# First part's layer out weights split once and kept in DRAM; a new order of scores, copies and sums at the beginning

## The chip, the cores and the metric

The kernel runs on one core of a Trainium2 chip. The metric is the device time of one execution in microseconds, the median of several runs.

## What is computed

Attention in chunks of 64, then a mixture of four experts (ReLU, weighted by normalised shares), then a gated layer. Cut to what matters:

```python
# q, k, v: (4, 8, 576, 64); chunks of 64 along the sequence
attn = softmax_over_chunk(q_c @ k_c.T / 8)            # eps 1e-9 in the sum
x = (attn @ v_c) -> (2304, 512)
# first part: 4 experts, w1 (4, 512, 1024), w2 (4, 1024, 512)
p = domain_probs / (domain_probs.sum(-1) + 1e-9)
x = sum_e p[:, e] * (relu(x @ w1[e]) @ w2[e])
# second part: w_gate, w_val (512, 1536), w_out (1536, 512)
g = x @ w_gate
out = (g * sigmoid(g) * (x @ w_val)) @ w_out
```

## The kernel before, in words

Every float32 operand of a matrix product is split into a high half h, which ScalarE (ACT) rounds to fp32r, and a low half l = source - h, which GpSimd (POOL) or VectorE (DVE) subtracts. A product is three matmuls: h*h, l*h and h*l. `split` (L103) writes the two halves; its lines are L104 (ACT) and L105 (DVE or POOL).

The 2304 tokens go in three passes of 768. A pass runs the first part's 16 sets of layer in weights (256 hidden columns each). Two sets make a group, so a pass has 8 groups in the first part. After the three passes come the three passes of the second part with 12 sets each. Layer in uses Strassen's seven products a set instead of eight (`PRODUCTS`, L59); the sums of weights that this needs are made by `w_sums` (L327). The first two sets of pass 0 are done plainly, without Strassen (`plain`, L504).

Layer out of a group (`layer2`, L516, the matmuls into y at L525, L527 and L529) runs while the next group's layer in runs: 72 matmuls of 512 columns, 18 after every second pair of products. It needs the group's four chunks of layer out weights, 128 rows x 512 columns each, split.

- Layer in weights: in pass 0 each set's raw weights are loaded (`fetch_w1`), summed on DVE, split, used, and the split halves are stored in DRAM (`make_w`, L342). From the third set of pass 1 on they are loaded split (`load_w`, L349).
- Layer out weights of the first part: in **every** pass `fetch_w2` (L406) loads a raw chunk (256 KB) and `split_w2` (L411) splits it on ACT and POOL into a tile of the pool w2 (7 tiles). The raw tiles have 2 buffers. Of the four chunks the last is split two products into the next group (L777, `W + 2`), since seven tiles do not hold two groups.
- Second part: its weights come as 64-bit numbers. `convert` (L358) turns a piece of 128 x 512 into float32 by operations on DVE, ACT and POOL; `make_set64` (L385) does a set with sums and splits, `make_wo` (L398) a chunk of layer out. They are generators: `run_tasks(2)` advances two of them by a step after each product. Four of the `make_wo` (`early`, L707) are put in at L799, when the last attention block is done in pass 0; the rest follows from the third set of pass 1 on (L801).

The order of every engine's instructions is the order in which this program issues them (`manual_schedule`); each engine and each DMA queue works in order. Nearly all DMAs are issued by SP. Work is put off by counting products: `later(d, f)` runs f after d more products.

The beginning (L594 to L695) does six attention blocks of 128 tokens for pass 0, stage by stage: `att_scores` (scores s on PE, maximum and subtraction on DVE, exponential on ACT), `att_turn` (transposes et, copy on ACT, row sums on DVE), `att_values` (av), `att_out` (transposes xt, high halves and a copy x on ACT, low halves on POOL or DVE). From the fifth round on, the plain products of the first two sets (banks of PSUM "z", "w", "x") stand between. `first_sums` (L302) makes the Strassen sums of the tokens, of four subtractions each two on DVE and two on POOL in turn.

The line that sets the order of stages in a round:

```python
stages((att_values, i - 1), (att_turn, i), (att_scores, i + 1), (att_out, i - 1))
```

## Time and profile before

| | us |
|---|---|
| median of 3 runs | 1325.85 (1323.39 to 1326.48) |
| the profiled execution, its own time | 1329.47 |
| its span, first to last instruction | 1327.7 |
| PE busy with matmuls | 1264.9 (95%) |
| DVE, ACT, POOL busy | 706.7, 549.1, 664.9 |
| mean granted TensorE clock | 0.979 |
| DMA | 296.16 MB, 223 GB/s over the span |

The granted clock is 1 at 2.4 GHz and 0.5 at 1.2 GHz; a mean between the two says how much of a stretch ran at either. PE's busy time counts slow and fast matmuls alike, so a stretch loses time in two ways: PE idle, and PE at the lower clock. Idle time of the other engines costs nothing by itself.

### The profile page before, as it was taken

Reading aid. Unit: us, or ns where it says so; the run is one execution under the profiler, and the core shown is the slowest. Engines: PE = TensorE matmul, PEld = TensorE weight load, DVE = VectorE, ACT = ScalarE, POOL = GpSimd, SP = SyncE. Lnnn points to the kernel's source line nnn. Section 1 sums busy time; section 2 is a strip of 40 time slices with the busy share of each in tenths; the row PEclk is TensorE's granted clock in tenths of the full one; section 3 lists DMA queues with packets and bytes.
Section 4 is the critical chain, followed back from the end, with each engine's and each line's share of the span. In section 5 each row is a group of like instructions: output and inputs, shape, how many; then the busy total and the mean of one; then the engine's idle time right before and its main releaser. Section 6 shows DMA issues by size and latency. Waiting matters only on the chain.

```text
span 1327.7 us, 19890 instructions
## 1 busy us (share of the span) xinstructions
PE 1264.9 (95%) x6724; PEld 1134.7 (85%) x6724; DVE 706.7 (53%) x1113; ACT 549.1 (41%) x1177; POOL 664.9 (50%) x632
## 2 busy tenths in 40 slices
PE   7799999987899899998999999999999999999998
PEld 6688888876788788997898888999999999999997
DVE  5567556465635656576764575344335433453343
ACT  3544444334443444445552444343444334343331
POOL 4644434376637667586675576133545423353231
PEclk8999999988899999999999999999999999999999
DMA  6376765656677686779687868475868775577641
GB/s 192 112 252 201 230 199 171 216 201 211 229 247 251 231 282 200 264 256 320 222 277 276 277 199 284 144 249 198 278 218 298 259 236 176 182 245 262 186 144 48
DMA packets 166885, 296.16 MB, mean 223 GB/s; under 512 B 17776, under 2 KB 43632, under 8 KB 166784
## 3 DMA queue, kind: packets, MB, share of 16 engines
q1 hardware_dynamic: 166752, 294.85, 66.8%
q8 instruction: 54, 0.88, 0.3%
q14 instruction: 47, 0.39, 0.1%
q0 software_dynamic: 32, 0.04, 0.0%
HBM read 219.84 MB, written 74.97 MB: 222 GB/s over the span
## 4 chain that ended last, share of the span: by engine, by line
PE 74%; DMA 6%; DVE 6%; POOL 5%; issue 4%; ACT 3%; SPq 1%; POOLq 0%; DVEq 0%; ACTq 0%
PE y L529 11%; PE y L527 11%; PE y L525 11%; PE lx L476 7%; PE lx L478 7%; PE lx L477 7%; PE lz L476 4%; PE lz L478 4%; PE lz L477 4%; PE lw L476 2%; PE lw L478 2%; PE lw L477 2%; POOL w_made L105 2%; DMA w<-w 2%; DMA raw_wo<-wo 1%
## 5 line engine op out<-in xcount | busy, mean ns | idle before, releaser
L105 POOL TENSOR_TENSOR w<-raw,w 128x512 fp32r<-128x512 f32 (+1 forms) x252 | 270.9, 1088 | 340.7 <-ACT w L104 297.3
L527 PE MATMUL y<-w,hh 128*128 128x512 f32 x792 | 314.9, 398 | 18.5 <-POOL w L105 18.5
L529 PE MATMUL y<-w,hl 128*128 128x512 f32 x792 | 315.4, 398 | 9.0 <-DVE hl L434 9.0
L525 PE MATMUL y<-w,hh 128*128 128x512 f32 x792 | 313.8, 396 | 6.5 <-ACT w L104 6.0
L527 PEld LDWEIGHTS y<-w,hh 128*128 128x128 f32 x792 | 150.0, 189 | 50.5 <-POOL w L105 23.0
L529 PEld LDWEIGHTS y<-w,hl 128*128 128x128 f32 x792 | 150.4, 190 | 42.5 <-DVE hl L434 10.5
L525 PEld LDWEIGHTS y<-w,hh 128*128 128x128 f32 x792 | 150.2, 190 | 36.5 <-ACT w L104 7.2
L108 POOL TENSOR_TENSOR hl<-sg,hh 128x384 fp32r<-128x384 f32 x72 | 79.6, 1112 | 199.4 <-ACT hh L451 191.0
L433 ACT ACTIVATE hh<-sum_p 128x384 fp32r<-128x384 f32 x92 | 48.3, 525 | 283.6 <-DVE sum_p L464 283.6
L464 DVE TENSOR_TENSOR sum_p<-lx,p 128x384 f32<-128x384 f32 x82 | 45.6, 556 | 167.4 <-PE lx L478 167.4
L546 DVE SCALAR_TENSOR_TENSOR acc<-y,prob,acc 128x512 f32<-128x512 f32 x126 | 90.9, 743 | 74.4 <-PE y L529 74.4
L104 ACT ACTIVATE w<-raw 128x512 fp32r<-128x512 f32 (+1 forms) x252 | 128.1, 522 | 3.0 <-DMA raw<-wo 1.9
L434 DVE SCALAR_TENSOR_TENSOR hl<-sum_p,hh 128x384 fp32r<-128x384 f32 x92 | 61.2, 666 | 60.3 <-ACT hh L433 60.3
L105 POOL TENSOR_TENSOR w_made<-raw,w_made 128x256 fp32r<-128x256 f32 x84 | 72.2, 876 | 9.6 <-ACT w_made L104 9.6
L460 ACT COPY u<-lx 128x384 f32<-128x384 f32 x82 | 39.1, 477 | 81.4 <-PE lx L478 81.0
L451 ACT ACTIVATE hh<-sg 128x384 fp32r<-128x384 f32 x72 | 38.0, 528 | 70.8 <-DVE sg L448 70.8
L464 DVE TENSOR_TENSOR sum_p<-lw,p 128x384 f32<-128x384 f32 x82 | 45.3, 553 | 36.5 <-PE lw L478 33.7
L476 PE MATMUL lw<-b21h,w 128*128 128x384 f32 x164 | 56.1, 342 | 6.9 <-DVE hl L434 5.5
L476 PE MATMUL lx<-t2h,w 128*128 128x384 f32 x164 | 56.9, 347 | 3.8 <-ACT p L460 3.7
L476 PE MATMUL lx<-t3h,w 128*128 128x384 f32 x164 | 57.7, 352 | 0.0
L478 PE MATMUL lx<-t3h,w 128*128 128x384 f32 x164 | 57.5, 351 | 0.0
L477 PE MATMUL lx<-t3l,w 128*128 128x384 f32 x164 | 57.4, 350 | 0.0
(233 smaller groups left out, 2842.5 us busy)
## 6 DMA issues: line engine op xcount, KB each, us to landing
w<-w SPq DMA_DIRECT2D x574, 256.0 KB, 4.4
raw<-w SPq DMA_DIRECT2D x96, 256.0 KB, 4.0
w<-w_made SPq DMA_DIRECT2D x84, 256.0 KB, 4.3
raw<-w SPq DMA_DIRECT2D x18, 512.0 KB, 3.9
raw<-wo SPq DMA_DIRECT2D x36, 256.0 KB, 4.6
sums<-x SPq DMA_DIRECT2D x40, 192.0 KB, 4.0
xt<-sums SPq DMA_DIRECT2D x40, 192.0 KB, 2.2
xraw_t<-xt SPq DMA_DIRECT2D x20, 384.0 KB, 4.2
```

What stands on the lines that cost most here:

```text
L104: nc.scalar.activation(h, src, AF.Copy)
L105: (lo or nc.vector).tensor_tensor(out=l, in0=src, in1=h.bitcast(F32), op=ALU.subtract)
L108: (eng or nc.vector).tensor_tensor(out=o, in0=a, in1=b, op=ALU.subtract)
L434: nc.vector.scalar_tensor_tensor(out=l, in0=src, scalar=0.0, in1=h.bitcast(F32), op0=ALU.max, op1=ALU.subtract)
L464: nc.vector.tensor_tensor(out=t, in0=ps, in1=snap.pop(name), op=ALU.add)
L476: nc.tensor.matmul(ps, w[:, 0, c], xh[:, k], start=f, stop=False, skip_group_check=True)
L477: nc.tensor.matmul(ps, w[:, 0, c], xl[:, k], start=False, stop=False, skip_group_check=True)
L478: nc.tensor.matmul(ps, w[:, 1, c], xh[:, k], start=False, stop=e, skip_group_check=True)
L525: nc.tensor.matmul(y, hh[:, c], w[:, 0], start=(j == 0), stop=False)
L527: nc.tensor.matmul(y, hh[:, c], w[:, 1], start=False, stop=False)
L529: nc.tensor.matmul(y, hl[:, c], w[:, 0], start=False, stop=(j == 3))
L546: nc.vector.scalar_tensor_tensor(out=sum_, in0=y, scalar=p, in1=sum_, op0=ALU.mult, op1=ALU.add)
```

## The change

It has three parts.

1. **Layer out weights of the first part.** In pass 0 a chunk, once split, is also stored in DRAM (`w2_d`, both halves, 512 KB), three products after its split. In passes 1 and 2 `fetch_w2` loads the two halves (512 KB) straight into the w2 tile, and `split_w2` does nothing. The tile is therefore taken when the load is issued, no longer at the split. From the last group of pass 0 on, the fourth chunk of every odd group has a tile of its own (`w2x_p`), so two groups fit, and the fourth chunk no longer waits for the next group.
2. **Conversions.** The four `early` conversions of second part layer out leave pass 0 and take their places in the list that starts in pass 1.
3. **The beginning.** Scores of the next block are issued ahead of this block's transposes, and the pieces of `att_scores` and `att_turn` on DVE and ACT are issued in a new order (`att_soft`, `att_sums`, `att_exp`). All four subtractions of `first_sums` go to DVE; the sums, splits and banks behind the plain products stand in a new order.

The diff, cut:

```diff
--- before.py
+++ after.py
@@ -98,6 +98,7 @@
 
     xt_d = [dram.tile([4, P, 2, TT], F32, name=f"xt_{s}") for s in range(2 * NPASS)]
     w_d = [dram.tile([NPROD, P, 2, 2 * P], F32, name=f"w_{n}") for n in range(NPAIRS + 2 * NPAIRS2)]
+    w2_d = [dram.tile([P, 2, DM], F32, name=f"w2_{c}") for c in range(4 * NG1)]
     wo_d = [dram.tile([P, DM], F32, name=f"wo_{c}") for c in range(F2 // P)]
 
     def split(h, l, src, lo=None):
@@ -232,11 +233,23 @@
                 )
         if next_in_place(a) is not None:
             att_load(next_in_place(a))
+        s["s"] = ps
+        if a >= BLOCKS:
+            att_soft(a)
+
+    def att_soft(a):
+        s = att[a]
+        ps = s.pop("s")
         mx = st_p.tile([P, H], F32, tag="mx", name=f"mx{a}")
         pool, how = (acc_p, dict(tag="acc")) if a < BLOCKS else (at_p, dict(tag="e", bufs=3))
         e = s["e"] = pool.tile([P, H, CH], F32, name=f"e{a}", **how)
         nc.vector.tensor_reduce(out=mx, in_=ps, op=ALU.max, axis=AX.X)
         nc.vector.tensor_tensor(out=e, in0=ps, in1=mx.unsqueeze(2).to_broadcast(ps.shape), op=ALU.subtract)
+        if a >= BLOCKS:
+            att_exp(a)
+
+    def att_exp(a):
+        e = att[a]["e"]
         nc.scalar.activation(e, e, AF.Exp, scale=SCALE)
 
     def transpose(ps, src):
@@ -253,6 +266,11 @@
         ps = transpose(att_ps(f"et{a}", where), s["e"])
         et = s["et"] = at_p.tile([P, H, CH], F32, tag="et", name=f"et{a}", bufs=1)
         nc.scalar.copy(et, ps)
+        if a >= BLOCKS:
+            att_sums(a)
+
+    def att_sums(a):
+        s = att[a]
         sm = st_p.tile([P, H], F32, tag="sm", name=f"sm{a}")
         nc.vector.tensor_reduce(out=sm, in_=s["e"], op=ALU.add, axis=AX.X)
         nc.vector.tensor_scalar_add(sm, sm, EPS)
@@ -305,9 +323,9 @@
         b1, b2 = x_first[0, j], x_first[1, j]
         d0, d1 = slice(0, 2), slice(2, 4)
         sub(b1[:, d0], b2[:, d0], b1[:, d0])
-        sub(b2[:, d0], b2[:, d1], b2[:, d0], nc.gpsimd)
+        sub(b2[:, d0], b2[:, d1], b2[:, d0])
         sub(b2[:, d1], b2[:, d1], b1[:, d0])
-        sub(b1[:, d1], b1[:, d1], b2[:, d1], nc.gpsimd)
+        sub(b1[:, d1], b1[:, d1], b2[:, d1])
 
     FIRST_PLACES = {"t1": (0, slice(0, 2)), "t3": (1, slice(0, 2)), "t2": (1, slice(2, 4)), "t4": (0, slice(2, 4))}
 
@@ -404,13 +422,27 @@
     raw2, w2op = {}, {}
 
     def fetch_w2(G, j):
-        part, _, g = part_of(G)
+        part, s, g = part_of(G)
+        if part == 1 and s > 0:
+            t = w2op[G, j] = w2_tile(G, j)
+            nc.sync.dma_start(t.bitcast(F32), w2_d[4 * g + j])
+            return
         r = raw2[G, j] = raw2_p.tile([P, DM], F32, tag="raw2", name=f"raw2_{G}_{j}")
         nc.sync.dma_start(r, w2[4 * g + j] if part == 1 else wo_d[4 * g + j])
 
+    def w2_tile(G, j):
+
+        pool = w2_p if G < NG1 - 1 or G % 2 == 0 or j < 3 else w2x_p
+        return pool.tile([P, 2, DM], F32R, tag="w2", name=f"w2_{G}_{j}")
+
     def split_w2(G, j):
-        t = w2op[G, j] = w2_p.tile([P, 2, DM], F32R, tag="w2", name=f"w2_{G}_{j}")
+        part, s, g = part_of(G)
+        if (G, j) not in raw2:
+            return
+        t = w2op[G, j] = w2_tile(G, j)
         split(t[:, 0], t[:, 1], raw2.pop((G, j)), lo=nc.gpsimd)
+        if part == 1:
+            later(3, lambda: nc.sync.dma_start(w2_d[4 * g + j], t.bitcast(F32)))
 
 
     hid = {}
@@ -465,7 +497,7 @@
         return t
 
     def bank(b, name):
-        return (psX if b == "x" else psL).tile([P, 512], F32, tag=b, name=name)[:, :TT]
+        return {"x": psX, "y": psY}.get(b, psL).tile([P, 512], F32, tag=b, name=name)[:, :TT]
 
     def half_k(ps, w, x, first, last):
 
@@ -635,14 +667,17 @@
             nc.gpsimd.tensor_tensor(out=prob, in0=prob, in1=sm.unsqueeze(2).to_broadcast(prob.shape), op=ALU.mult)
 
         def stages(*some):
-            for stage, a in some:
+            for stage, a, *w in some:
                 if 0 <= a < BLOCKS:
-                    stage(a, where())
+                    stage(a, *w)
+
+
 
         for i in range(-1, BLOCKS + 1):
             if i >= HALF + 1:
                 plain(*pieces.pop(0), "zw"[i % 2])
-            stages((att_values, i - 1), (att_turn, i), (att_scores, i + 1), (att_out, i - 1))
+            stages((att_values, i - 1, where()), (att_scores, i + 1, where()))
+            stages((att_turn, i, where()), (att_soft, i + 1), (att_sums, i), (att_out, i - 1, where()), (att_exp, i + 1))
             if i == 0:
                 shares()
             elif i == 1:
@@ -659,38 +694,37 @@
                 w2_p = ctx.enter_context(tc.tile_pool(name="w2", bufs=7, reuse_waits="tile"))
                 fetch_w2(0, 0)
                 fetch_w2(0, 1)
-            elif i == 6:
-                first_sums(0)
-                first_split("t2", 0)
-                w_sums(raw1[2], nc.gpsimd)
 
         del raw1[0], raw1[1]
         fetch_w1(3)
-        plain(*pieces.pop(0), "x")
-        first_sums(1)
-        first_split("t2", 1)
+        plain(*pieces.pop(0), "w")
+        first_sums(0)
         make_w(2, 0)
         make_w(2, 1)
-        plain(*pieces.pop(0), "x")
+        plain(*pieces.pop(0), "y")
+        first_sums(1)
+        w_sums(raw1[2], nc.gpsimd)
+        first_split("t2", 0)
+        plain(*pieces.pop(0), "y")
         first_sums(2)
+        first_split("t2", 1)
         first_split("t2", 2)
         make_w(2, 2)
+        make_w(2, 3)
+        plain(*pieces.pop(0), "z")
+        for j in range(HALF):
+            first_split("t1", j)
         split_w2(0, 0)
         split_w2(0, 1)
         fetch_w2(0, 2)
         fetch_w2(0, 3)
-        plain(*pieces.pop(0), "z")
-        for j in range(HALF):
-            first_split("t1", j)
-        make_w(2, 3)
-        plain(*pieces.pop(0), "w")
+        plain(*pieces.pop(0), "x")
+        make_w(2, 4)
+        make_w(2, 5)
         for j in range(HALF):
             first_split("t3", j)
-        plain(*pieces.pop(0), "x")
-        make_w(2, 4)
         split_w2(0, 2)
         split_w2(0, 3)
-        make_w(2, 5)
         for j in range(HALF):
             first_split("t4", j)
 
@@ -704,12 +738,9 @@
         tasks, running = [], []
 
         make64 = []
-        early = [make_wo(c) for c in range(4)]
         for q in range(NPAIRS2):
             for m in range(2):
-                make64.append(make_set64(q, m))
-                if 2 * q + m >= 4:
-                    make64.append(make_wo(2 * q + m))
+                make64 += [make_set64(q, m), make_wo(2 * q + m)]
 
         def run_tasks(n):
             while len(running) < n and tasks:
@@ -773,8 +804,9 @@
 
                 W = NPROD * sum(group_of(k) == group_of(n) for k in range(len(sets)))
                 for j in range(4):
+                    last = W + 2 if group_of(n) < NG1 - 1 else 5 + j * W // 4
                     later(1 + j * W // 4, lambda G=group_of(n), j=j: fetch_w2(G, j))
-                    later(5 + j * W // 4 if j < 3 else W + 2, lambda G=group_of(n), j=j: split_w2(G, j))
+                    later(5 + j * W // 4 if j < 3 else last, lambda G=group_of(n), j=j: split_w2(G, j))
             if last_of_pass(n + 1) and i == 5:
                 for k in range(3):
                     x_fetch(p + 1, k)
@@ -794,9 +826,10 @@
                     at_cm.close()
                     y_places.append((psA, "a"))
                     xt_p = ctx.enter_context(tc.tile_pool(name="xt", bufs=3, side="right"))
+                    w2x_p = ctx.enter_context(tc.tile_pool(name="w2x", bufs=1, side="right"))
                     raw64_cm = ExitStack()
                     raw64_p = raw64_cm.enter_context(tc.tile_pool(name="raw64", bufs=2, side="right"))
-                    tasks += [x_sums(1)] + early
+                    tasks.append(x_sums(1))
             if o == (NPAIRS + 2, 1):
                 tasks += [x_sums(2)] + make64
             elif o == (2 * NPAIRS + 3, 1):
```

### Where instructions move

Three places, row by row as the program's order has them. In a row stands the line, the operation, the tile written, the tiles read, and the shape; "x8" is eight in a row.

PE in the beginning, from the first scores on (s scores, et transposed exponentials, av values, xt transposed outputs; plz is the first plain product). Before:

```order
L230 MATMUL s_222<-kbd_158,q_196 64x128 x8
L244 MATMUL et_240<-ident,e_236 128x128 x4
L230 MATMUL s_252<-kbd_160,q_200 64x128 x8
L268 MATMUL av_275<-vbd_159,et_245 64x128 x8
L244 MATMUL et_287<-ident,e_266 128x128 x4
L230 MATMUL s_299<-kbd_162,q_206 64x128 x8
L244 MATMUL xt_313<-ident,e_236 128x128 x4
L268 MATMUL av_334<-vbd_161,et_292 64x128 x8
```

Now:

```order
L231 MATMUL s_254<-kbd_190,q_228 64x128 x8
L231 MATMUL s_272<-kbd_192,q_232 64x128 x8
L257 MATMUL et_285<-ident,e_268 128x128 x4
L286 MATMUL av_307<-vbd_191,et_290 64x128 x8
L231 MATMUL s_319<-kbd_194,q_238 64x128 x8
L257 MATMUL et_328<-ident,e_293 128x128 x4
L257 MATMUL xt_344<-ident,e_268 128x128 x4
L286 MATMUL av_366<-vbd_193,et_333 64x128 x8
```

The next block's scores now stand ahead of this block's et, where they stood behind it.

POOL near the end of pass 0, sets 13 and 14 (raw_5_3 is the last raw chunk of layer out of group 5, raw_6_0 the first of group 6; raw_13 is the layer in weights of set 13; wo a conversion; sums_1_1 the token sums of pass 1). Before:

```order
L380 TENSOR_TENSOR neg_wo_2946<-neg_wo_2946,raw_wo_2887 128x512
L381 TENSOR_TENSOR top_wo_2945<-top_wo_2945,neg_wo_2946 128x512
L105 TENSOR_TENSOR w_5_3_3042<-raw_5_3_2898,w_5_3_3042 128x512
L105 TENSOR_TENSOR w_2_3046<-raw_13_2863,w_2_3046 128x256
L105 TENSOR_TENSOR w_3_3062<-raw_12_2656,w_3_3062 128x256
L105 TENSOR_TENSOR w_5_3086<-raw_13_2863,w_5_3086 128x256
L105 TENSOR_TENSOR w_6_0_3124<-raw_6_0_2999,w_6_0_3124 128x512
```

Now:

```order
L109 TENSOR_TENSOR sums_1_0_2940<-sums_1_0_2940 128x384
L106 TENSOR_TENSOR w_5_3_3087<-raw_5_3_2952,w_5_3_3087 128x512
L106 TENSOR_TENSOR w_2_3091<-raw_13_2916,w_2_3091 128x256
L106 TENSOR_TENSOR w_3_3107<-raw_12_2707,w_3_3107 128x256
L106 TENSOR_TENSOR w_5_3130<-raw_13_2916,w_5_3130 128x256
L106 TENSOR_TENSOR w_6_0_3166<-raw_6_0_3046,w_6_0_3166 128x512
```

The two rows of the conversion ahead of group 5's last split are gone.

SP in pass 1 (w_83, w_84 the stored halves of sets' layer in weights; before: raw_11_1 a raw chunk of layer out, 128x512; now: w_11_0 the split halves of one, 128x1024; wv and wo the 64-bit weights of the second part). Before:

```order
L351 DMA w_5_4756<-w_83 128x512
L409 DMA raw_11_0_4775<-w 128x512
L351 DMA w_0_4777<-w_84 128x512
L360 DMA raw_0_1_4781<-wg 128x1024
L351 DMA w_1_4817<-w_84 128x512
L351 DMA w_6_4830<-w_83 128x512
L409 DMA raw_11_1_4847<-w 128x512
```

Now:

```order
L369 DMA w_5_4729<-w_83 128x512
L428 DMA w_11_0_4749<-w_12_117 128x1024
L369 DMA w_0_4751<-w_84 128x512
L378 DMA raw_1_1_4753<-wv 128x1024
L369 DMA w_1_4788<-w_84 128x512
L369 DMA w_6_4798<-w_83 128x512
L419 DMA wo_138<-top_wo_4697 128x512
L428 DMA w_11_1_4813<-w_13_118 128x1024
```

The load of a chunk keeps its place in the queue; it is twice as large and takes its w2 tile there.

## Rows read from the trace of the kernel before

**Rows 1.** Busy time in eight stretches: window, PE, PEld, DVE, ACT, POOL, clock, DMA share, GB/s

```profile
0.00:14.00 14.00, 9.39 (x69) 8.26 (x70) 6.49 (x15) 3.13 (x4) 7.54 (x20) 0.78 0.72 219
14.00:44.00 30.00, 24.24 (x222) 19.80 (x223) 16.39 (x34) 14.31 (x35) 11.47 (x17) 0.93 0.59 171
44.00:73.00 29.00, 22.34 (x141) 19.96 (x140) 18.82 (x31) 14.50 (x39) 23.88 (x28) 0.88 0.29 92
73.00:240.00 167.00, 167.00 (x1073) 145.08 (x1073) 103.89 (x182) 70.19 (x166) 67.67 (x77) 1.00 0.67 216
240.00:322.00 82.00, 66.52 (x311) 56.88 (x310) 47.20 (x70) 32.16 (x75) 47.46 (x48) 0.92 0.57 196
322.00:380.00 58.00, 53.53 (x254) 47.83 (x253) 32.90 (x43) 25.09 (x55) 35.62 (x32) 0.91 0.72 239
380.00:830.00 450.00, 429.13 (x2114) 382.20 (x2113) 276.74 (x400) 204.12 (x437) 293.45 (x269) 0.98 0.76 257
830.00:1327.00 497.00, 492.71 (x2553) 454.70 (x2551) 204.26 (x343) 185.59 (x369) 177.81 (x145) 1.00 0.63 209
```

**Rows 2.** PE's waits between 240 and 830 us: total us, times, longest

```profile
PE y L527 <- POOL w L105: 17.2, 10, 3.4
PE y L529 <- DVE hl L434: 9.0, 4, 4.2
PE y L525 <- ACT w L104: 6.0, 2, 5.2
```

**Rows 3.** The same waits between 380 and 830 us, one row

```profile
PE y L527 <- POOL w L105: 13.3, 8, 3.4
```

**Rows 4.** Timeline of PE in the beginning: start, us, instruction, [idle before <- releaser]

```profile
14.85 1.09 PE L230 MATMUL s<-kbd,q 128*64 128x128 f32 x16
...
18.71 1.09 PE L230 MATMUL s<-kbd,q 128*64 128x128 f32 x16
...
26.12 0.45 PE L476 MATMUL plz<-b11h,w 128*128 128x384 f32 x1 [1.87 <-ACT b11h L291]
...
63.14 0.69 PE L476 MATMUL lw<-b21h,w 128*128 128x384 f32 x1 [5.47 <-DVE hl L434]
...
72.79 0.50 PE L525 MATMUL y<-w,hh 128*128 128x512 f32 x1
```

**Rows 5.** Timeline of DVE in the beginning

```profile
52.73 0.43 DVE L108 TENSOR_TENSOR x<-x,x 128x256 f32<-128x256 f32 x1 [2.71 <-POOL x L108]
53.70 0.56 DVE L105 TENSOR_TENSOR t2l<-x,t2h 128x256 fp32r<-128x256 f32 x1 [0.54 <-ACT t2h L104]
...
59.90 2.72 DVE L105 TENSOR_TENSOR t1l<-x,t1h 128x256 fp32r<-128x256 f32 x3
```

**Rows 6.** Timeline of ACT in the beginning: the split of a chunk

```profile
64.23 0.94 ACT L104 ACTIVATE w<-raw 128x512 fp32r<-128x512 f32 x2 [0.87 <-DMA raw<-w]
```

**Rows 7.** Timeline of DVE and POOL late in pass 0: a conversion

```profile
309.23 0.43 DVE L367 TENSOR_SCALAR top_wo<-raw_wo 128x512 f32<-128x512 f32 x1 [6.17 <-DMA raw_wo<-wo]
...
271.17 1.51 POOL L380 TENSOR_TENSOR neg_wo<-neg_wo,raw_wo 128x512 f32<-128x512 f32 x1
272.75 1.32 POOL L381 TENSOR_TENSOR top_wo<-top_wo,neg_wo 128x512 f32<-128x512 f32 x1
```

**Rows 8.** Timeline of PE late in pass 0: two of its waits

```profile
275.54 0.49 PE L527 MATMUL y<-w,hh 128*128 128x512 f32 x1 [2.84 <-POOL w L105]
...
315.69 0.80 PE L525 MATMUL y<-w,hh 128*128 128x512 f32 x1 [5.24 <-ACT w L104]
```

**Rows 9.** Groups by line and shape, 380 to 830 us: busy, mean ns | idle before

```profile
L105 POOL TENSOR_TENSOR w<-raw,w 128x512 fp32r<-128x512 f32 x53 | 71.7, 1353 | 111.5 <-ACT w L104 84.1 <-DVE hl L434 15.8 <-DMA w<-w 11.6
...
L104 ACT ACTIVATE w<-raw 128x512 fp32r<-128x512 f32 x54 | 33.4, 619 | 0.0
```

**Rows 10.** DMA issues of the page: the load of split layer in weights

```profile
w<-w SPq DMA_DIRECT2D x574, 256.0 KB, 4.4
```

## The prediction

> **What bounds the kernel now.** I read the windows first [rows 1]. In each row the reader should see two losses of PE: the stretch less PE's busy time, and the stretch times one less the clock (time at 1.2 GHz does half the work, and the mean clock says how much of it there was). From 73 to 240 us PE is never idle and at the full clock; there the kernel is bound by its matmuls, and no edit off PE can gain. From 830 us on it loses 4.3 us, all of it near the end. The losses stand elsewhere:
>
> - 0 to 14 us: idle 4.6, clock 3.1, together 7.7.
> - 14 to 73 us: idle 5.8 + 6.7, clock 2.1 + 3.5, together 18.0.
> - 240 to 322 us: idle 15.5, clock 6.6, together 22.0.
> - 322 to 380 us: idle 4.5, clock 5.2, together 9.7.
> - 380 to 830 us: idle 20.9, clock 9.0, together 29.9.
>
> That is 87 us, and no more than this can be won. Next come PE's waits [rows 2, 3]: between 240 and 830 us the largest is layer out's matmul (y) for a low half of its weights, which POOL writes: 17.2 us in ten waits, 13.3 of it after 380 us. Layer out's other two waits are for a high half on ACT (6.0) and for hidden low halves on DVE (9.0). For the cause of a wait I then looked at the timeline of the engine that releases it [rows 5 to 7].
>
> **The change, part by part.** The sum is made against the profiled execution's own time, 1329.47 us, which is 3.6 above the median of the runs; the forecast takes the same gain off the median.
>
> *The beginning (14 to 73 us).* Before, the scores of the next block stand behind this block's et, which waits for maximum, subtraction and exponential. So a block takes 18.71 - 14.85 = 3.86 us [rows 4]. With the scores ahead of et, DVE and ACT work beside PE, and a block is bounded by PE's four pieces, 1.09 for s as in the row, about the same for av, and under 0.7 each for et and xt: some 3.4 us by estimate. Over five blocks that is 2 us. The stalls at the first plain product (1.87 us idle, [rows 4]) shrink only in part, since its low halves still come from the last xt through ACT and DVE. The token sums go back and forth between DVE and POOL: one wait of DVE for POOL is 2.71 us [rows 5], behind POOL's weight sums. Four subtractions on DVE alone are 4 x 0.43 = 1.7 us a place instead of about 3.2 from one place's first to its last. Three places come 4 to 5 us earlier, and this chain ends at the 5.47 us stall of PE at 63.14 [rows 4] and at the 1.2 GHz stretch behind it, part of the 3.5 us. But the late chunks of layer out are still fetched into two raw buffers behind POOL's splits of the first two, and ACT, which splits them in order ahead of a copy that PE needs, already waits for such a load [rows 6]. With everything earlier that wait grows, and a part of the stall comes back there. So of 18.0 I take **10**; bounds 4 (only the block pace and one short stall) and 14. Nothing in 0 to 14 us is taken: what ends those waits are the first loads.
>
> Here a rule weighs against the move to DVE. Three low halves on DVE took 2.72 us beside POOL's work, 0.91 each, where one by itself took 0.56 [rows 5]. So 12 subtractions and 6 low halves could each be 0.35 longer, 18 x 0.35 = 6 us; the beginning would give 4, and the sum below would be 31 instead of 37. I leave it as a rival, since before the change the POOL pieces of the sums met DVE as well. The Trainium skill says why (SBUF — State Buffer, section "SBUF: two separate sides"): an operation of DVE with two SBUF inputs and one of GpSimd take a shared pair of ports in turn, and whoever comes second is blocked for the whole of the other's instruction. By that rule it is the 31.
>
> *Conversions leave pass 0 (240 to 322 us).* Four conversions stand here. DVE waits 6.17 us in order for the raw load of one [rows 7], and everything behind it, ACT's split of a chunk among it, comes late: PE waits 5.24 us [rows 8]. Two POOL pieces of another, 1.51 + 1.32 us [rows 7], stand right ahead of a chunk's low half, and PE waits 2.84 [rows 8]: the very length of the two. Up to 240 us the same sets without conversions cost PE no wait at all, though there the attention blocks gave POOL and DVE more time a set. Of 22.0 us I take **18**; bounds 11 (clock and the smaller waits stay) and 22. From 322 to 380 us the cause is mostly pass 0's own weight sums on DVE, which stay; I take **2**, bounds 0 and 5.
>
> *Chunks loaded split in passes 1 and 2 (380 to 830 us).* 64 splits go; 53 of POOL's pieces lie in this stretch, 71.7 us of POOL, and 33.4 of ACT [rows 9]. By themselves they cost nothing; what counts is PE's 13.3 us behind them [rows 3] and a like share of the clock loss, 13.3 / 20.9 x 9.0 = 5.7. The fourth chunk no longer stands right ahead of its use. Of 19 I take **14**; bounds 8 (other POOL pieces make the next weights late) and 21 (some of DVE's waits go as well).
>
> *What it adds.* The four conversions now come in passes 1 and 2. Bounds: nothing, as PE's other losses there, 29.9 - 19 = 11 us over 32 pieces of the same kind, are 0.3 a piece; and 22, what four cost late in pass 0. I take **3**, near the rows of their new place. The list of conversions gets longer, not denser: two still run at a time.
>
> DMA: 32 stores of 512 KB in pass 0 and 64 loads larger by 256 KB, 16.8 MB each. At full share the rows give 216 / 0.67 = 322 and 257 / 0.76 = 338 GB/s [rows 1], so 52 and 50 us of the engines' time, spread over about 280 and 500 us: shares of 0.86 or so in both. It fits, but what stands behind such a transfer comes 0.8 us later (0.26 MB at 338 GB/s). If one in four of 64 loads passed that on to PE, 12 us; if none, 0. I take **4**. The stores also put 32 waits for POOL into SP's queue, in a pass whose loads have lasted without a wait of PE from 73 to 240 us; I cost them at nothing there, their cover being the six products by which weights are asked for ahead.
>
> SP: a load now waits for its w2 tile, until 18 matmuls of layer out of two groups before are through. At 497 us for 2553 matmuls [rows 1] those are 3.5 us. Once a group SP is held until then; the split weights behind it have six products of lead and land in 4.4 us [rows 10]. So it is costed at nothing; if the lead is used up, see the second rival. What goes: SP's waits for POOL to free the two raw buffers.
>
> The sum: 10 + 18 + 2 + 14 - 3 - 4 = 37 us. 1329.5 - 37 = 1292.5 for the profiled execution; from the median, 1325.85 - 37 = **1289**.
>
> **The rivals.**
>
> 1. *DVE becomes the beginning's bound*, by the taking of turns above. For it: 0.91 against 0.56 [rows 5]. Against: POOL's share of the sums goes. Beginning 4, sum 31, 1295. Chance 0.15.
> 2. *SP is held and loads come late: slower.* Place: passes 1 and 2, the first chunk of each of 16 groups. If the six products of lead are not there, because SP was late before, each hold passes its 3.5 us on to PE: 16 x 3.5 = 56 us, 1289 + 56 = 1345. It decides from 37 / 16 = 2.3 us a group. For it: the queue is one and in order, and the DMA share rises. Against: loads land in 4.4 us, and SP loses its old waits. Chance 0.08.
> 3. *The conversions take their stalls along.* In passes 1 and 2 they are as dear as in pass 0: 22 instead of 3, sum 18, 1308. For it: POOL and DVE are as busy there, 0.65 and 0.61 of the stretch [rows 1]. Against: 32 such pieces cost PE at most 11 us there now. Chance 0.15.
> 4. *It doesn't do what it says.* PE's next matmuls wait for the next POOL piece in line instead, the 14 are not won, and the conversions take their stalls along: 37 - 14 - 19 = 4, 1322. Chance 0.04.
>
> **How the numbers follow.** The forecast has what is left, 0.58. What a measurement of this kernel can tell from no change is about 0.3%, 4 us. Faster by more than that: forecast, rivals 1 and 3, 0.58 + 0.15 + 0.15 = 0.88. Within it: rival 4, 0.04. Slower: rival 2, 0.08. The range's low end has all upper bounds and nothing added: 14 + 22 + 5 + 21 = 62, so 1264. The high end has the lower bounds with the dear side of what is added, short of the conversions' 22: 4 + 11 + 0 + 8 - 3 - 8 = 12, so 1314. It holds the forecast, rivals 1 and 3, and leaves out rivals 2 and 4, 0.12, and some tails.
>
> **What would show it.** In the profile after:
>
> - the first layer out matmul, at 72.79 before [rows 4], comes near 63; if near 69, rival 1;
> - PE's idle and clock loss in pass 0 after attention is under 5 us, and no wait there is put down to ACT's or POOL's split of a chunk;
> - in passes 1 and 2 no split of 128x512 is left on POOL, and layer out waits for a low half on POOL in the second part at most;
> - PE's waits for DMA of split weights, if any, stay under 5 us in sum; if they stand once a group, rival 2.
>
> The forecast is wrong if PE still loses over 45 us between 73 and 830 us, or if the gain stands where no term puts it.

## The result and the profile after

| | before | after |
|---|---|---|
| median of the runs on this chip, us | 1325.53 (1323.39 to 1326.48) | 1276.95 (1276.67 to 1277.32) |
| the profiled execution, its own time | 1329.47 | 1277.32 |
| its span | 1327.7 | 1275.6 |
| PE busy | 1264.9 (95%) | 1244.0 (98%) |
| POOL busy | 664.9 | 568.5 |
| mean granted clock | 0.979 | 0.993 |
| DMA moved, MB | 296.16 | 329.71 |

The ratio is 0.9636, with a 95% interval of 0.9619 to 0.9652: 48.6 us faster by the medians. The forecast was 1289, from 1264 to 1314: the direction and the range hold, and the gain is 11.6 us larger than the 37 of the sum.

The windows of the profile after, cut as those of before where the place in the program is the same (window, its length, PE, PEld, DVE, ACT, POOL, clock, DMA share, GB/s):

```profile
0.00:14.00 14.00, 10.38 (x104) 8.88 (x106) 8.61 (x18) 4.38 (x8) 7.86 (x20) 1.00 0.75 229
14.00:44.00 30.00, 24.49 (x217) 21.58 (x214) 15.85 (x35) 15.35 (x38) 11.88 (x17) 0.94 0.64 192
44.00:73.00 29.00, 21.61 (x137) 19.40 (x137) 21.83 (x38) 14.31 (x36) 20.41 (x24) 0.88 0.33 95
...
240.00:322.00 82.00, 81.17 (x419) 72.80 (x418) 50.39 (x70) 35.44 (x82) 55.64 (x55) 1.00 0.85 298
322.00:380.00 58.00, 53.48 (x264) 47.23 (x263) 27.42 (x44) 20.49 (x44) 17.73 (x17) 0.94 0.78 279
...
380.00:830.00 450.00, 444.35 (x2226) 399.24 (x2225) 270.23 (x425) 189.54 (x403) 222.57 (x220) 1.00 0.84 301
```

Against [rows 1]: from 240 to 322 us PE's loss falls from 22.0 to 0.8; from 380 to 830 us it falls from 29.9 to 5.7 (450 - 444.35, with the clock at 1.00 to two decimals). The 29.9 is some 2.5 too high: its 9.0 of clock comes from a mean of 0.98 over 450 us, and windows of 50 us give 0.97, 0.97, 0.99 and 0.94 in four of nine and 1.00 in the others, which is 6.5. From 14 to 73 us the idle time and the clock look about as before (18.0 and 18.2 us lost); the first 14 us, of which the forecast took nothing, lose 3.6 instead of 7.7.

The program runs ahead of its old times, so windows alone mislead; places in the program are better. I take the same four places in both timelines: the first matmul of layer out, the last transpose of attention, the stall at the change from pass 0 to 1, and the first sigmoid of the second part. Of PE after:

```profile
62.48 0.69 PE L508 MATMUL lx<-t2h,w 128*128 128x384 f32 x1 [7.39 <-ACT p L492]
...
68.07 0.50 PE L557 MATMUL y<-w,hh 128*128 128x512 f32 x1
...
244.36 0.63 PE L257 MATMUL xt<-ident,e 128*128 128x128 f32 x4 [0.83 <-DVE e L293]
...
331.34 0.79 PE L561 MATMUL y<-w,hl 128*128 128x512 f32 x1 [3.30 <-DVE hl L466]
```

and of ACT after:

```profile
843.39 0.53 ACT L473 ACTIVATE sg<-sum_p 128x384 f32<-128x384 f32 x1
```

In the trace before the first stands at 72.79 [rows 4], the other three here:

```profile
248.65 0.63 PE L244 MATMUL xt<-ident,e 128*128 128x128 f32 x4 [0.83 <-DVE e L275]
...
357.87 0.80 PE L529 MATMUL y<-w,hl 128*128 128x512 f32 x1 [4.23 <-DVE hl L434]
...
894.08 0.53 ACT L441 ACTIVATE sg<-sum_p 128x384 f32<-128x384 f32 x1
```

So the lead is 4.7, then 4.3, 26.5 and 50.7 us, and 52.1 at the end of the span. The differences say where it was won: **beginning 4.3, late pass 0 22.2, passes 1 and 2 24.2, the rest 1.4**. (The traces differ by 52.1 and the medians by 48.6, since the profiled run of before lay 3.9 above its median.)

The 24.2 holds most of that excess. From the stall at the change of pass to the first sigmoid the profiled execution of before takes 536.2 us. Two kernels below that split chunks there just as before, a1_begin and a2_wo, take 529.4 and 529.6 in theirs, and a1_begin's lay 3.1 below its median. The change takes 512.1. So by medians passes 1 and 2 gained some 20, by estimate (24.2 less 3.9).

The waits of PE after, between 380 and 830 us (total us, times, longest), are four, 5.6 us in sum, and have nothing of a weight in them:

```profile
PE y L561 <- DVE hl L466: 2.9, 2, 1.7
PE y L557 <- ACT acc L597: 1.6, 1, 1.6
PE x1t L257 <- DVE acc L578: 0.7, 1, 0.7
PE lx L508 <- ACT p L492: 0.4, 1, 0.4
```

Before, the same stretch had the row for POOL [rows 3] and smaller ones, of which the two largest are:

```profile
PE y L529 <- DVE hl L434: 3.3, 1, 3.3
PE lw L476 <- DMA w<-w: 1.4, 2, 1.1
```

The row for POOL, 13.3 us, is gone, with the splits that made it. It is most of what went: PE's idle time there fell by 15.2 us (20.9 to 5.7), so the other waits fell by 2 in all. SP's queue shows the hold that the second rival feared, L428 waiting for layer out's last matmul, 16 times, as many as passes 1 and 2 have groups, and the same queue's waits for POOL to free raw tiles (164.2 us in 50 times before) shrunk to L431's:

```profile
SPq L369 <- PE lx L510: 93.0, 75, 3.0
...
SPq L428 <- PE y L561: 41.0, 16, 7.6
...
SPq L431 <- POOL w L106: 24.3, 8, 15.6
```

### The profile page after: what moved, and what is told of

Read it like the earlier page. It is cut to its first block, busy times and chain, and to the rows that moved or that the text cites. A ratio compares the mean times of both kernels' runs of the same rounds, so it can differ in the third digit from the quotient of the medians.

```text
span 1275.6 us, 19749 instructions
## 1 busy us (share of the span) xinstructions
PE 1244.0 (98%) x6724; PEld 1123.0 (88%) x6724; DVE 680.9 (53%) x1119; ACT 518.8 (41%) x1113; POOL 568.5 (45%) x562
## 2 busy tenths in 40 slices
DMA packets 171492, 329.71 MB, mean 258 GB/s; under 512 B 18288, under 2 KB 44144, under 8 KB 171392
## 4 chain that ended last, share of the span: by engine, by line
PE 86%; DVE 5%; DMA 3%; ACT 2%; issue 1%; SPq 1%; POOL 1%; DVEq 0%; POOLq 0%; ACTq 0%
PE y L561 13%; PE y L557 13%; PE y L559 13%; PE lx L508 8%; PE lx L510 8%; PE lx L509 8%; PE lz L508 4%; PE lz L510 4%; PE lz L509 4%; PE lw L510 2%; PE lw L508 2%; PE lw L509 2%; PE av L286 1%; PE s L231 1%; ACT hh L465 1%
## 5 line engine op out<-in xcount | busy, mean ns | idle before, releaser
L106 POOL TENSOR_TENSOR w<-raw,w 128x256 fp32r<-128x256 f32 (+1 forms) x188 | 184.9, 1000 | 207.9 <-ACT w L105 178.0
L106 POOL TENSOR_TENSOR w_made<-raw,w_made 128x256 fp32r<-128x256 f32 x84 | 67.6, 814 | 71.4 <-ACT w_made L105 65.0
L105 ACT ACTIVATE w<-raw 128x256 fp32r<-128x256 f32 (+1 forms) x188 | 88.7, 490 | 7.6 <-DMA raw<-w 6.4
L398 POOL TENSOR_TENSOR neg<-neg,raw 128x512 f32<-128x512 f32 x24 | 31.7, 1322 | 113.6 <-DMA w<-w 51.5
L508 PE MATMUL lz<-t1h,w 128*128 128x384 f32 x164 | 56.1, 342 | 0.0
L508 PE MATMUL lx<-t3h,w 128*128 128x384 f32 x164 | 56.0, 342 | 0.0
L510 PE MATMUL lx<-t3h,w 128*128 128x384 f32 x164 | 55.9, 341 | 0.0
```

What stands on the lines that cost most here:

```text
L105: nc.scalar.activation(h, src, AF.Copy)
L106: (lo or nc.vector).tensor_tensor(out=l, in0=src, in1=h.bitcast(F32), op=ALU.subtract)
L508: nc.tensor.matmul(ps, w[:, 0, c], xh[:, k], start=f, stop=False, skip_group_check=True)
L510: nc.tensor.matmul(ps, w[:, 1, c], xh[:, k], start=False, stop=e, skip_group_check=True)
```

## The experiments

My theory after the result was: each of the three parts acts by itself, late pass 0 through the conversions, passes 1 and 2 through the splits, and the beginning gave little because ACT's splits of late chunks stand ahead of a copy that PE needs. Rivals: the chunks' new tile and place rather than the missing splits; DVE slowed by POOL in the beginning; conversions that are dear in their new place; traffic or SP's holds that eat a part of the gain. Eleven kernels were run, in three groups, each beside the kernel before on one chip. A difference "against the change" is taken between medians; as the kernel before had 1326.2 to 1326.5 beside these groups and 1325.5 beside the change, up to 1 us of such a difference can be the chip.

**One part at a time.** The kernel before with the third part of the change (order and sums at the beginning), nothing else:

```diff
+            stages((att_values, i - 1, where()), (att_scores, i + 1, where()))
+            stages((att_turn, i, where()), (att_soft, i + 1), (att_sums, i), (att_out, i - 1, where()), (att_exp, i + 1))
...
-        sub(b2[:, d0], b2[:, d1], b2[:, d0], nc.gpsimd)
+        sub(b2[:, d0], b2[:, d1], b2[:, d0])
```

> The beginning's new order alone; layer out chunks and conversions as before. Theory: the three parts work in separate stretches and add up, and the beginning is worth what the two traces show at the last transposes of attention, 248.65 - 244.36 = 4.3 us: 1321. Rival: it is worth the 10 of the forecast and the other parts take some back: 1315.

Measured: 1320.93 against 1326.5, ratio 0.9960 (0.9940 to 0.9979), about 5.6 us. First layer out matmul and last transpose stand about where they stand in the change (68.0 and 243.9, against 68.07 and 244.36). The beginning is worth about 5, not 10.

The kernel before with the four conversions moved to the list of pass 1:

```diff
-        early = [make_wo(c) for c in range(4)]
...
+                make64 += [make_set64(q, m), make_wo(2 * q + m)]
...
-                    tasks += [x_sums(1)] + early
+                    tasks.append(x_sums(1))
```

> The four conversions moved from pass 0 to passes 1 and 2, nothing else. Theory: the stalls between 240 and 322 us go (22 us) and each conversion costs under 1 us in its new place: 1304 to 1307. Rival: conversions take their stalls along, 5.5 us each: 1320 to 1326.

Measured: 1300.68, ratio 0.9811 (0.9787 to 0.9835), 25.8 us. The windows of this kernel, late in pass 0 and in passes 1 and 2:

```profile
240.00:322.00 82.00, 81.17 (x417) 72.62 (x416) 52.04 (x72) 36.88 (x86) 55.07 (x55) 1.00 0.70 236
...
380.00:830.00 450.00, 433.73 (x2142) 388.25 (x2141) 286.04 (x418) 210.10 (x447) 300.12 (x274) 0.99 0.76 261
```

From 240 to 322 us PE loses 0.8 instead of 22.0. In passes 1 and 2, where four more conversions now run, it does not lose more than before (16.3 idle against 20.9, and against 18.5 in a1_begin, which has the old conversions). The third rival of the prediction falls.

The kernel before with the chunks stored and loaded split (the first part of the change, with its eighth tile):

```diff
+        if part == 1 and s > 0:
+            t = w2op[G, j] = w2_tile(G, j)
+            nc.sync.dma_start(t.bitcast(F32), w2_d[4 * g + j])
+            return
```

> Chunks stored split in pass 0 and loaded split in passes 1 and 2, with the eighth tile; beginning and conversions as before. Theory: passes 1 and 2 gain about 24 us, the stores cost nothing: 1301. Rival: the stores meet the conversions' loads in pass 0 and make their stalls longer, or the gain after 330 us needed the conversions' move: 1308 or more.

Measured: 1303.56, ratio 0.9830 (0.9811 to 0.9848), 22.9 us. Its windows:

```profile
240.00:322.00 82.00, 64.48 (x307) 54.73 (x306) 46.53 (x69) 31.90 (x75) 47.35 (x47) 0.92 0.68 241
...
380.00:830.00 450.00, 445.53 (x2232) 400.90 (x2231) 260.89 (x414) 184.64 (x394) 215.29 (x216) 1.00 0.84 297
```

Late pass 0 keeps its whole loss, while in passes 1 and 2 PE is idle for only 4.5. The three parts give 5.6 + 25.8 + 22.9 = 54.3 by themselves and 48.6 together: nearly additive, each mainly in its own stretch.

**Splits, or the fourth chunk's place?** The change, but passes 1 and 2 load raw chunks and split them; the eighth tile stays, nothing is stored:

```diff
-        if part == 1 and s > 0:
-            t = w2op[G, j] = w2_tile(G, j)
-            nc.sync.dma_start(t.bitcast(F32), w2_d[4 * g + j])
-            return
...
-        if part == 1:
-            later(3, lambda: nc.sync.dma_start(w2_d[4 * g + j], t.bitcast(F32)))
```

> As the changed kernel, but passes 1 and 2 load raw chunks and split them on ACT and POOL, and nothing is stored; the eighth tile stays, so the fourth chunk is split four products after its load and not in the next group. Theory: the work of 64 splits and SP's waits for raw buffers cost most of the gain in passes 1 and 2: 1288 to 1300. Rival: the fourth chunk's late place was the whole of it: 1277 to 1281.

Measured: 1292.38, ratio 0.9750 (0.9731 to 0.9768), 15.4 slower than the change. Its window of passes 1 and 2:

```profile
380.00:830.00 450.00, 433.48 (x2141) 386.06 (x2140) 277.73 (x415) 209.73 (x446) 297.67 (x273) 0.99 0.77 261
```

and the wait that came back in SP's queue:

```profile
SPq L426 <- POOL w L105: 106.1, 39, 15.5
```

PE's wait for POOL's low halves is back too, 5.2 us in 4 waits. The fair comparison for this kernel is a2_wo, which has the same conversions and the same splits without the eighth tile. From the stall at the change of pass to the first sigmoid, a2_wo:

```profile
333.91 0.80 PE L529 MATMUL y<-w,hl 128*128 128x512 f32 x1 [4.43 <-DVE hl L434]
...
863.54 0.53 ACT L441 ACTIVATE sg<-sum_p 128x384 f32<-128x384 f32 x1
```

and this kernel:

```profile
329.46 0.79 PE L554 MATMUL y<-w,hl 128*128 128x512 f32 x1 [3.30 <-DVE hl L459]
...
858.97 0.53 ACT L466 ACTIVATE sg<-sum_p 128x384 f32<-128x384 f32 x1
```

That is 529.6 and 529.5 us: the fourth chunk's new place won nothing there in these two executions. By medians at most some 3 us are left for it, if the other two parts add up (1326.5 - 5.6 - 25.8 = 1295.1). It is the splits that count, with the raw tiles that hold up SP; these two come and go together here, and no run parts them.

**The beginning: POOL beside DVE, or ACT's order?** The change with two of four subtractions back on POOL:

```diff
-        sub(b2[:, d0], b2[:, d1], b2[:, d0])
+        sub(b2[:, d0], b2[:, d1], b2[:, d0], nc.gpsimd)
...
-        sub(b1[:, d1], b1[:, d1], b2[:, d1])
+        sub(b1[:, d1], b1[:, d1], b2[:, d1], nc.gpsimd)
```

> As the changed kernel, with first_sums alternating between DVE and POOL as before. Theory: PE's next matmuls wait for ACT, which waits for late chunk loads, so where the sums run hardly matters: within 2 us of 1277. Rival (DVE is slowed by POOL): faster than 1277 by 2 to 6 us. Other rival (the move was the gain): 1280 or more.

Measured: 1278.99, ratio 0.9642 (0.9627 to 0.9656), 2.0 slower than the change by medians, with overlapping intervals. In the trace the first layer out matmul comes at 70.27, and the wait for ACT's copy is 9.5 us, where it is 7.2 to 8.1 in the seven traces that have the beginning of the change. That DVE meets POOL does cost DVE time (below), but giving POOL the work back is no gain.

The change with the splits of the third and fourth chunk put off behind the first products:

```diff
-        split_w2(0, 2)
-        split_w2(0, 3)
...
+        later(1, lambda: split_w2(0, 2))
+        later(2, lambda: split_w2(0, 3))
```

> As the changed kernel, but chunks 2 and 3 of the first group are split one and two products later, so that ACT's copy which frees the bank no longer stands behind their late loads. Theory: PE's wait of 7.4 us before the third product shrinks to about 4 (the next bound is the exponential of block 6, behind DVE's weight sums), and with it the 1.2 GHz stretch: 1272 to 1274. Rival (the wait only moves to layer out, which needs these chunks): 1276 to 1278.

Measured: 1274.13 (1273.08 to 1275.35), ratio 0.9599 (0.9583 to 0.9615), 2.8 faster than the change: it **beats both kernels**. ACT in the change, ahead of the copy that PE waits for:

```profile
58.98 0.63 ACT L105 ACTIVATE w<-raw 128x512 fp32r<-128x512 f32 x1 [1.84 <-DMA raw<-w]
60.52 0.63 ACT L105 ACTIVATE w<-raw 128x512 fp32r<-128x512 f32 x1 [0.91 <-DMA raw<-w]
61.05 1.01 ACT L105 ACTIVATE t4h<-x 128x256 fp32r<-128x256 f32 x3
61.97 0.46 ACT L492 COPY p<-lx 128x384 f32<-128x384 f32 x1
```

and in this kernel:

```profile
55.98 1.01 ACT L105 ACTIVATE t4h<-x 128x256 fp32r<-128x256 f32 x3
56.90 0.46 ACT L492 COPY p<-lx 128x384 f32<-128x384 f32 x1
```

The copy comes 5 us earlier, PE's longest wait for it falls from 7.4 to 3.4, and the first layer out matmul comes at 65.57. Not all of it is this edit's: the first stretch, to 44 us, went somewhat better in this trace too (25.23 us of PE against 24.49, where the waits for the first loads differ from run to run), and the first layer in product stood 1.1 us earlier ahead of the stall (49.52 against 50.58). So of the 2.5 us at the first layer out matmul some 1.4 are the edit's in this pair of traces.

A third try at the same stall, the first set's layer in weights fetched one attention block later (`if a == 3:` for `if a == 2:`, so that SP sends attention's loads first):

> As the changed kernel, but the first raw weights (512 KB) are asked for behind the fourth block's q and k instead of ahead of them. Theory: the scores of the fourth block, which wait 2.9 us for k, come 1.5 to 2 us earlier, and the 1.2 GHz stretch behind them is shorter: 1273 to 1275 if nothing later takes it back. Rival: it is taken back at the wait for chunks, whose time is set by POOL's splits: 1276.5 to 1278.

Measured: 1279.43 (1276.88 to 1281.22), ratio 0.9640 (0.9621 to 0.9658). The wait for attention's loads went from 4.0 to 2.0, that for ACT's copy to 8.5. In this trace PE ran slower from 14 to 44 us (clock 0.83 against 0.94), and the first layer in product came at 53.75 against 50.58. No gain; why the clock was lower is not shown.

**What the change adds.** Each split chunk loaded twice into its tile, to double the traffic:

```diff
-            nc.sync.dma_start(t.bitcast(F32), w2_d[4 * g + j])
+            for _ in range(2):
+                nc.sync.dma_start(t.bitcast(F32), w2_d[4 * g + j])
```

> As the changed kernel, but each of the 64 loads of split chunks in passes 1 and 2 is issued twice, 33.5 MB more. Theory: the DMA engines have room there (0.85 of the time busy), SP's hold costs nothing, so 64 more loads cost 0 to 8 us: 1277 to 1285. Rival (DMA is at its limit): 33.5 MB at 340 GB/s are 99 us over 510 us, above what is free, and PE pays 20 us or more: 1297 or more.

Measured: 1441.21, ratio 1.0857 (1.0837 to 1.0876), 164 us slower, far from both. The kernel did not test what I meant: the second load writes the tile that the first writes, so SP waits until the first has landed, with everything queued behind it. PE's waits in this kernel:

```profile
PE lx L509 <- DMA w<-w: 64.9, 38, 5.9
PE lz L509 <- DMA w<-w: 15.2, 13, 2.6
PE lw L509 <- DMA w<-w: 10.0, 9, 2.7
```

and the longest of the waits in SP's queue:

```profile
SPq L429 <- DMA w<-w: 375.7, 77, 8.2
```

It is the second rival's mechanism at work, SP held until PE's loads come late: 164 / 64 = 2.6 us for each added load. The waits are only a part of it; the clock from 380 to 830 us is 0.92. In the change SP is held 41.0 us in 16 waits at no cost that a wait of PE shows; held 375.7 us in all, it runs through the lead of six products.

The traffic by itself then: one more load of 256 KB behind each, into a tile that nobody reads, so 16.8 MB more:

```diff
+            u = spare_p[0].tile([P, DM], F32, tag="u", name=f"u_{G}_{j}")
+            nc.sync.dma_start(u, w2_d[4 * g + j][:, 0])
```

> The change, with one more load of 256 KB behind each of the 64 loads of split chunks in passes 1 and 2, into a tile of its own that nobody reads: the 16.8 MB that the change itself adds to loads there, once more, and this time no load waits for the one just ahead of it. Theory (that traffic is hidden, six products of lead are enough): within 3 us of the change, 1274 to 1280, no wait of PE for DMA of weights over 2 us. Rival (the prediction's 4 us for traffic was near, the DMA share of 0.85 leaves little): 4 to 12 us slower, 1281 to 1289, with PE's waits for DMA spread over passes 1 and 2.

Measured: 1281.97 (1278.58 to 1283.64), ratio 0.9658 (0.9634 to 0.9682), 5.0 slower than the change, the single runs 1.6 to 6.7, with overlapping intervals. Neither side is clean. No wait of PE names a DMA of weights, though the DMA share from 580 to 680 us is 0.95. The trace loses most of its time at one spot, the change from pass 1 to 2. The 20 us there in the change, its window and PE's wait:

```profile
680.00:700.00 20.00, 18.32 (x90) 15.99 (x89) 14.41 (x24) 8.07 (x18) 8.84 (x7) 1.00 0.85 310
...
689.84 0.50 PE L561 MATMUL y<-w,hl 128*128 128x512 f32 x1 [1.68 <-DVE hl L466]
```

The same 20 us with the spare loads:

```profile
680.00:700.00 20.00, 16.96 (x67) 13.80 (x66) 11.78 (x21) 8.71 (x17) 5.25 (x4) 0.83 0.94 329
...
693.50 0.80 PE L563 MATMUL y<-w,hl 128*128 128x512 f32 x1 [2.89 <-DVE hl L468]
```

DVE there waits in order for the raw load of a conversion, 7.75 us in the change and 9.93 here; PE's wait for a hidden low half grows from 1.68 to 2.89, and the clock of these 20 us is 0.83 (1.4 us more idle and 3.4 of clock). SP is also held in this kernel, for its one spare tile (32.4 us in 18 waits), so its 5.0 is an upper price of the traffic more than the traffic's alone.

Three conversions done twice in their new place:

```diff
+                if 2 * q + m < 3:
+                    make64.append(make_wo(2 * q + m))
```

> The change, with three of the second part's layer out conversions done twice in the list that starts in pass 1 (the same result written again). It doubles the cost that the prediction put on the new place of four conversions. Theory (there they cost PE nothing, since two generators run at a time whatever the list's length): within 2 us of the change, 1275 to 1279. Rival (the dear bound, 22 us for four, 5.5 each): 16 us slower, 1293. The prediction's own value, 3 for four, would give 1279.

Measured: 1277.54 (1276.05 to 1279.34), ratio 0.9625 (0.9602 to 0.9648), 0.6 slower than the change, within what can be told. The conversions cost PE nothing that can be told in passes 1 and 2.

The change with the four conversions back in pass 0:

```diff
+        early = [make_wo(c) for c in range(4)]
...
-                    tasks.append(x_sums(1))
+                    tasks += [x_sums(1)] + early
```

> The change, with the four early conversions put back into pass 0. Theory (pass 0 has no room for them because POOL and DVE make its weights there, whatever is done to chunks and beginning): about 22 to 25 us slower, 1299 to 1302, the stretch from 240 to 322 us again with a mean clock of about 0.92 and layer out's waits for POOL's split. Rival (the stalls came from conversions and late tiles together, so the new order frees part of them): under 15 us slower, under 1292.

Measured: 1301.3 (1296.98 to 1303.51), ratio 0.9803 (0.9777 to 0.9829), 24.4 slower. The window late in pass 0 is that of before again [rows 1]:

```profile
240.00:322.00 82.00, 65.21 (x312) 55.90 (x311) 46.47 (x69) 30.40 (x71) 48.54 (x48) 0.92 0.70 241
```

and so are PE's waits in the whole of this kernel [rows 2, 8]:

```profile
PE y L557 <- ACT w L105: 6.0, 1, 6.0
...
PE y L559 <- POOL w L106: 5.7, 3, 4.3
```

So the same four conversions are dear in pass 0 whatever is done to chunks and beginning, and free in passes 1 and 2.

## Why the prediction was right, and where its sizes were off

*Late pass 0, 18 + 2 forecast: right.* The traces give 22.2 up to the stall at the change of pass, the conversions alone 25.8, and putting them back 24.4. The upper bound of 22 was the better value: with the conversions went the clock loss too (0.92 to 1.00), which I had let stay in part. One check failed in its letter: between 322 and 380 us 8 us are still lost, since the stall for hidden low halves at the change of pass stays (4.23 us before, 3.30 after) with a stretch at a lower clock behind it.

*Passes 1 and 2, 14 - 3 - 4 = 7 forecast, 24.2 found in the traces, some 20 by medians: the step that failed.* The row of waits behind the splits and its share of the clock loss were read rightly, as 13.3 + 5.7 = 19. What failed is what was then taken off. "Of 19 I take 14", because other POOL pieces might make the next weights late: they did not, the row went whole, no wait for POOL took its place, and the clock loss went whole (9.0 as the prediction read it, 6.5 in windows of 50 us). Then 7 were to be given back, and nearly nothing was: the conversions, put at 3, measure 0.6 for three of them in c4_wo_twice; the traffic, put at 4, shows in no wait of PE, and as much again costs 5.0 at most, at another place than "one in four of 64 loads". Taken back with all else in place (a4_place), the splits cost 15.4; taken away alone (a3_chunks), with the fourth chunk's place, they give 22.9. Either is far above 7.

*The beginning, 10 forecast, 4.3 found: near its lower bound, but not where it was put.* One step that failed is the one on the stall at 63.14: "a part of the stall comes back there". It came back whole, as 7.39 us at 62.48 behind ACT's copy in place of 5.47 behind a hidden low half [rows 4]. The first layer in product, ahead of the stall, and the product lx<-t2h behind it show this best. Before:

```profile
55.31 0.45 PE L476 MATMUL lx<-b11h,w 128*128 128x384 f32 x1 [0.52 <-DVE hl L434]
...
67.27 0.69 PE L476 MATMUL lx<-t2h,w 128*128 128x384 f32 x1
```

and the first of them after (the second, at 62.48, is shown above):

```profile
50.58 0.33 PE L508 MATMUL lx<-b11h,w 128*128 128x384 f32 x1
```

From one to the other it is 11.96 us before and 11.90 after. So the whole lead was won ahead of the stall, and all that was forecast for the stall failed to come. The earlier token sums only moved PE's wait to ACT, which stood in order at the splits of the third and fourth chunk, whose raw loads SP sends when POOL has split the first two. The prediction had that chain [rows 6] and gave it too little. b2_split_later takes it away and wins part of it back.

The other step that failed is "Nothing in 0 to 14 us is taken: what ends those waits are the first loads." The longest wait of before there was not for a load:

```profile
8.72 1.11 PE L244 MATMUL et<-ident,e 128*128 128x128 f32 x4 [2.17 <-ACT e L240]
```

With the next scores ahead of et it is gone. The first 14 us lose 3.4 to 4.3 us in the seven traces with the beginning of the change, and 7.7, 6.5 and 6.1 in before, a2_wo and a3_chunks. So most of the beginning's gain stands where no term of the forecast put it, one of the prediction's own signs of being wrong; that its size fell near the lower bound is luck.

*Rival 1* would have been read as true from its mark: the first layer out matmul came at 68.07, near 69, and the beginning gave the 4 that it named. Yet with work moved back to POOL the same way from lx<-b11h to lx<-t2h takes 14.0 us, where it takes 11.7 to 12.6 in six of these seven traces, and b2_split_later shortens it to 7.9 by ACT's order alone: the mark did not tell the two apart. The slowing itself is real. Four subtractions of one place beside POOL's splits and weight sums, and those of a later place with POOL idle, on DVE after:

```profile
43.46 0.89 DVE L109 TENSOR_TENSOR x<-x,x 128x256 f32<-128x256 f32 x1
44.45 0.77 DVE L109 TENSOR_TENSOR x<-x 128x256 f32<-128x256 f32 x1
45.33 1.65 DVE L109 TENSOR_TENSOR x<-x,x 128x256 f32<-128x256 f32 x2
...
50.44 0.42 DVE L109 TENSOR_TENSOR x<-x,x 128x256 f32<-128x256 f32 x1
50.89 0.42 DVE L109 TENSOR_TENSOR x<-x 128x256 f32<-128x256 f32 x1
51.35 0.89 DVE L109 TENSOR_TENSOR x<-x,x 128x256 f32<-128x256 f32 x2
```

That is 3.31 us against 1.73, for the first place; the next one takes 2.15. So the meeting costs the subtractions some 2 us in all, not the 6 that the rival put on them and six low halves, because POOL's sums had ended by the last place (at 48.46). (The prediction's 0.56 for a low half "by itself" [rows 5] was not by itself: POOL ran a subtraction from 53.24 to 53.98. With POOL idle one takes 0.42, at 49.64 after.) The Trainium skill (SBUF — State Buffer, section "SBUF: two separate sides") says that the one who comes second is blocked for the whole of the other's instruction; the doubled times agree with it, and the run says that here it was not what decided.

*Rival 2* had its hold where it was put, 16 times, up to 7.6 us instead of 3.5, and passed nothing on: the lead was there. b3_twice shows that the mechanism is sound. *Rival 3* and *rival 4* fall by a2_wo and a3_chunks.

That the sum came as near as 11.6 us is in part luck: the beginning was put some 5 too high, and passes 1 and 2 some 13 too low. A slip in the range changes nothing: its high end takes 8 for the traffic, where the dear side worked out was 12, which would give 1318.

## What to carry to other kernels

Where work off the critical path is taken away, start from the wait that names it, with the clock loss that goes with it. Here that came to 19, and some 20 came. Then ask of each amount taken off it which row shows it: the wait that another piece was to take over did not arise, and the work and the traffic that were to cost 7 fell where PE did not wait for them. The same piece of work can cost 6 us in one pass and nothing in the next, so ask of a new place what its engines make there: in pass 0 they make the weights that PE needs next, later these come from DRAM. That reason is argued from the rows and was not tried by itself. And a stall whose releaser comes earlier moves to the next engine in order: follow it to the engine that is late next, and take that one's early work out of the way.

## What the runs showed that I had not expected

- Holding the SP queue is free up to a point and then very dear: 16 holds, 41.0 us in all, cost nothing; in c3_early_back even 67.2 us in 17 holds, the longest 17.3, left PE without a wait for a DMA of weights; with 64 more loads that each write a tile still being loaded the kernel is 164 us longer, at a DMA share below that of the change (0.79 from 380 to 930 us, against 0.84 from 380 to 830 there).
- A DMA share of 0.91 to 0.95 (325 to 342 GB/s in each 100 us from 380 to 780, c1_spare) left PE without one wait for a DMA of weights; what became late was a raw load that DVE takes in order.
- A wait of 1.68 us at the change from pass 1 to 2 left the granted clock at 1.00 in its 20 us, one of 2.89 us at the same place went with 0.83: of the 4.8 us lost there more, 3.4 were the clock, not the wait. It is one pair of executions.
- The same code can differ by 7 us in one stretch: passes 1 and 2, with splits as before, took 536.2 us in one execution and 529.4 in another. A gain read by places from one pair of traces needs the medians beside it.
